# First chunk of a Mamba-2 scan with a maxout FFN: B by token turned on TensorE instead of loaded, x in two transfers, and every engine's order rewritten

## The chip, the cores and the metric

The kernel runs on one core of a Trainium2 chip. A core has TensorE (PE; its weight loads are a row of their own, PEld), VectorE (DVE), ScalarE (ACT), GpSimd (POOL), and SyncE (SP), which here issues nearly all DMAs. Every engine works through its own list of instructions in order, and waits at an instruction until the semaphores that it needs have come. The metric is device microseconds of one execution; the kernel before has a median of 245.2 us in 3 runs.

## The reference, cut to what matters

The first part is a scan over 768 tokens for 4 batches x 8 heads (head width 32, state width 16):

```python
for c in range(nc):                       # chunks of tokens
    cum = np.cumsum(log(a)[chunk])
    M = (C @ B.T) * exp(cum_i - cum_j) * causal
    y = M @ x + (C @ state) * exp(cum_i)
    state = exp(cum[-1]) * state + (B * exp(cum[-1] - cum_j)).T @ x
```

The second part takes the 3072 tokens with 256 channels (heads side by side) through a maxout layer: `h = max(y @ w1, y @ w2, y @ w3)` with 768 columns each, `out = h @ w_out`. The four weights come as 64-bit floats.

## The kernel before, in words

**Chunks.** The 768 tokens of each batch are six chunks of 128 tokens, each worked as two halves of 64 (`W`). A chunk of the scan gives y for 4 x 128 tokens; its FFN follows, mixed in with the scan of the next chunk. Chunk 0 is worked by code of its own (all names with `first_`), since nothing can run before it.

**The order is written out by hand.** `OPENING` is one list of words for chunk 0 and the preparation of the weights. `FIRST`, `SECOND`, `STEADY` and `LAST` are the lists for the chunks after it, 12 strings each, one for each unit of the up-projection (6 blocks of 128 columns x 2 products). Each word calls one function, which puts its instructions at the end of the engines' lists; a word with `+` continues a function that stopped at a `yield`. So the place of a word sets the order on each engine, and an engine whose next instruction waits lets everything behind it wait.

Words of `OPENING` that matter, with lines of the profile:

- `em` (L656, L662) decay from the middle of the chunk; `cm` (L666) C times that decay, "Cd0".
- `fj0`, `bt0` (L451, L458 to L466) the decay from each token to the end, turned to tokens on partitions; `R`, `S0`, `S1` (L385 to L405) the exponents of the decay between tokens, `x0` to `x3` (L418) their exp for each batch.
- `tC`, `tB` (L589) VectorE transposes C and B; `cp` (L676) copies C with every other head zeroed, in two halves, "CP"; `sc0` (L601) the scores; `p0` to `p3` (L607) scores times decay.
- `bT` (L617) turns the first 64 tokens of B back on TensorE; `bm` (L623) times the decay, "Bm"; `Am` (L637) the state in mid-chunk, `mid` (L645) its masked copy.
- `ya0` to `ya3` (L799, copy L814), `yc0` to `yc3` (L828, L799, copies L838 and L840): y of the first and of the second 64 tokens, put into `yT`. `yc` starts with Cd0 times mid (L828).
- `z` adds one filler product (L413) to the next bank of PSUM that is opened; fillers compute nothing that is used.
- `clip log run hl1 hl2` (L331, L336, L342, L482 to L489) make the running sums of log a for chunks 1 to 5, split in three bf16 parts. These go out to DRAM (`sums`, L492) and come back as `left` (L504, word `rows`) and `right` (L498), the operands of the exponents of chunk 1 (`X02`, `X24`, L522). `minus1` (L326) fills `right` with its constant rows on ScalarE. `fj`, `bt` (L352, L361) the decays to the end for chunks 1 to 5.
- `fetch` issues the next transfer of 512 KB of weights (L205); `decode` and `sign` turn its 64-bit words to fp32: two ScalarE operations (L224, L225), three on VectorE (L227, L230, L237), and one on POOL (L240).
- `bu0:1` and the like: next step of the difference of two weights ("d", L917) and of its splitting in parts ("wH", "wL", "wS", L865 to L905). `g` (L1067) turns a block of w2; with wo it makes "fold" (L1081).
- `m0` (L877) the first two up products with the first 64 tokens of each batch; `n0` and `n1` complete them; `n2` to `n11` (L1325) are the other up products of chunk 0, in plain fp32; `q` (L1108) its down products. From chunk 1 on the parts H, L and S are used (L981, L1022, L1140).
- `Bd0`, `A0` (L699, L714) the state at the end of chunk 0. It needs B by token for all 128 tokens, which `LB0` loads (L144, 256 KB in rows of 64 bytes).
- `y`, `v`, `Y` (L769, L790, L779): y of a later chunk; between its two parts ScalarE reads one column of the bank (`seen`), and the second part waits for that.

Before `OPENING`, the transfers of C and B of chunk 0 (L155, four each), one weight, x of chunk 0 in one piece, and two more weights (`NFETCH`) are issued in the text of the kernel:

```python
    load_first("C")
    load_first("B")
    fetch()
    load(0, "x")
    for _ in range(NFETCH):
        fetch()
```

In the plans, `Z` is one unit of the up-projection: it opens one of the two `up` banks of PSUM, finishes the unit before (`late`, L1022) and, for every second unit, VectorE takes the maximum (`h`, L1031) that frees the bank. `hS`, `wS` (L865), `hL` (L1044) are parts of h and of weights. `d` is a down product, `t`, `c`, `e`, `s`, `A` steps of the next chunk's scan, `X` and `W` its exponents, `E` their exp with the mask on POOL (L531, L536).

Of the kernel before, what the change touches and what calls it, by code (L numbers as in the profile page):

```python
# [20 lines left out]
def kernel(  # L21
# [20 lines left out]
    nc = tc.nc  # L42
# [25 lines left out]
    NFETCH = 2  # L68
# [79 lines left out]


# [544 lines left out]

    def scan_bd(c):
# [7 lines left out]
    def scan_state(c):  # L703
# [5 lines left out]
        for b in range(NB):  # L709
            for r in range(NP):  # L710
                h = b * NH + 2 * r
                for u in us:
# [3 lines left out]
                        lhsT=st["Bd"][rows, h:h + 2].rearrange("j h n -> j (h n)"),  # L716
# [498 lines left out]
    def first_word(w):  # L1215
# [21 lines left out]
        elif w == "bT":  # L1237
            first_turned_b()
# [73 lines left out]
    def first_group(n):  # L1312
# [36 lines left out]
    )  # L1349
    FIRST = [  # L1350
        "Z e 1 bu1:1 load bu1:1 1 bu1:1 bu0:1 bu1:1",
        "Z q X04 E E E bu0:1",
        "Z E q q t c 1",
        "Z q bo:1 bo:1",
        "Z bu1:1 s 1 1 1",
        "Z bu2:1 bu2:1 1 g",
        "Z bu2:1 bu2:1 G6 G6",
        "Z A 1",
        "Z r r r bu2:1 r W04 E E 1 bo:1 bo:1 bo:1 bo:1",
        "Z y d d",  # L1360
        "Z d d d E E d v Y 1",
        "Z 1 1 1 d d",
    ]
    SECOND = [
        "Z e d d t c bo:1 bo:1 d load d",
        "Z s",
        "Z 1 1 1 1 1 d d",
        "Z d d",
        "Z A 1",
        "Z d d",  # L1370
        "Z d 1 d",
        "Z W04 d E E",
        "Z d d d y v",
        "Z d d E E",
        "Z d d Y 1",
        "Z 1 1 d d 1",
    ]
    STEADY = [
        "Z 1 t d d d",
        "Z c E load d",  # L1380
        "Z d 1 d s 1",
        "Z 1 d 1 1 d A E",
        "Z d d",
        "Z d e d 1",
        "Z d d W04 E 1 1 E",
        "Z d y d d E",
        "Z E d v 1",
        "Z Y 1 1 d",
        "Z d 9 d d E E",
        "Z d 1 1 d",  # L1390
    ]
    LAST = [
        "Z d d",
        "Z d d d d d d",
        "Z d d",
        "Z d d",
        "Z d d",
        "Z d d d d",
        "Z l l",
        "Z l",  # L1400
        "Z l l l l",
        "Z l l l",
        "Z l l",
        "Z l l l",
# [33 lines left out]
    def act(c, word):  # L1438
# [77 lines left out]
        "R S0 S1 x0 x1 x2 x3 tC tB cp minus1 fj0 bt0 sc0 p0 p1 p2 p3 bT bm Am mid em cm ya0 ya1 ya2 ya3 yc0 yc1 yc2 yc3 m0 clip "  # L1516
        "log run hl1 hl2".split())
    for word in OPENING.split():
# [20 lines left out]
        elif word == "Bd0":  # L1539
            scan_bd(0)  # L1540
# [64 lines left out]
```

## Time and profile before

| | us |
|---|---|
| median of 3 runs (244.84 to 245.66) | 245.2 |
| the profiled execution | 246.31 |
| its span, first to last instruction | 244.6 |
| PE busy | 235.1 |
| DVE busy | 145.5 |
| ACT busy | 134.2 |
| POOL busy | 115.4 |

The profile is one execution. Rows give a start in us from the span's start, a length, the engine, the line of the kernel, the operation, what it writes and reads and the number of instructions merged in the row; in brackets the idle time of the engine ahead of it and what ended it. Rows of waits give total, times, longest. SPq is the issue of DMAs by SyncE. The profiled execution lies 1.1 us above the median; 1.7 us of it lie outside the span. DMA moved 17.88 MB in 70987 packets, of which 64460 were under 512 bytes.

### The profile page before, as it was taken

How to read it: one execution, taken by the hardware profiler on the slowest of the kernel's cores; microseconds unless marked ns; L12 is line 12 of the kernel's file. 1: busy time of each engine (PE TensorE's matmuls, PEld its weight loads, DVE VectorE, ACT ScalarE, POOL GpSimd, SP SyncE). 2: the span in 40 equal slices, each digit the busy share in tenths (PEclk: the TensorE clock that was granted, in tenths of full speed). 3: DMA queues.
4: the chain of work that ended last, by engine and by line, in shares of the span. 5: the costliest groups of instructions: out<-in, count | busy, mean ns of one | idle time of the engine just before them, and what ended most of it. 6: DMA issues, size and time to landing. Idle time of an engine off the chain costs nothing.

```text
span 244.6 us, 7115 instructions
## 1 busy us (share of the span) xinstructions
PE 235.1 (96%) x3024; PEld 186.6 (76%) x3024; DVE 145.5 (59%) x231; ACT 134.2 (55%) x254; POOL 115.4 (47%) x111
## 2 busy tenths in 40 slices
PE   8798999999989999999999999999999999999994
PEld 3456475566768878888878888888888888998993
DVE  5988998946698254787533963456764362333232
ACT  4788684903845474555547545663726364344352
POOL 5024566686696759374765323863315123122231
PEclk9889999999999999999999999999999999999999
DMA  3999996023939121290021450020000020002002
GB/s 84 206 352 381 150 184 138 3 46 62 126 68 136 12 87 36 62 128 4 0 91 40 93 69 3 3 82 6 0 3 3 3 88 0 0 0 88 1 1 86
DMA packets 70987, 17.88 MB, mean 73 GB/s; under 512 B 64460, under 2 KB 67884, under 8 KB 70956
## 3 DMA queue, kind: packets, MB, share of 16 engines
q1 hardware_dynamic: 70556, 17.19, 32.4%
q8 instruction: 23, 0.38, 0.6%
q10 hardware_dynamic: 400, 0.25, 0.3%
q14 instruction: 8, 0.07, 0.1%
HBM read 14.14 MB, written 3.29 MB: 71 GB/s over the span
## 4 chain that ended last, share of the span: by engine, by line
PE 90%; DVE 4%; issue 2%; DMA 1%; ACT 1%; SPq 1%; DVEq 0%; POOL 0%; POOLq 0%
PE up L981 22%; PE o L1140 19%; PE up L1022 11%; PE up L1325 7%; PE y L790 3%; PE o L1108 3%; PE near L1193 3%; PE y L769 3%; PE fold L1081 2%; PE s L748 2%; PE A L714 2%; PE up L877 2%; PE o L1121 1%; PE cross L1193 1%; PE up L966 1%
## 5 line engine op out<-in xcount | busy, mean ns | idle before, releaser
L1044 POOL TENSOR_TENSOR hL<-h,hH 128x512 fp32r<-128x512 f32 (+1 forms) x31 | 39.4, 1272 | 80.9 <-ACT hH L1043 79.7
L988 ACT ACTIVATE up<-up 128x512 f32<-128x512 f32 x60 | 35.3, 588 | 49.7 <-PE up L981 47.1
L865 DVE SCALAR_TENSOR_TENSOR hS<-hL,hH 128x512 fp32r<-128x512 f32 (+1 forms) x31 | 28.6, 921 | 31.1 <-POOL hL L1044 31.1
L981 PE MATMUL up<-yH,wH 128*128 128x512 f32 x116 | 39.5, 422 | 1.1 <-DVE h L1031 1.1
L1031 DVE SCALAR_TENSOR_TENSOR h<-up,m 128x512 f32<-128x512 f32 x29 | 20.0, 689 | 30.2 <-PE up L1022 28.1
L1022 PE MATMUL up<-yS,wS 128*128 128x512 f32 x116 | 36.6, 396 | 0.0
L981 PE MATMUL up<-yL,wL 128*128 128x512 f32 x116 | 36.0, 391 | 0.0
L240 POOL TENSOR_TENSOR w<-w_u,w_r 128x512 uint32<-128x512 uint32 x12 | 16.4, 1366 | 27.4 <-DVE w_r L237 27.4
L1027 ACT COPY m<-up 128x512 f32<-128x512 f32 x29 | 17.0, 586 | 18.9 <-PE up L1022 17.1
L1022 PEld LDWEIGHTS up<-yS,wS 128*128 128x128 f32 x116 | 21.4, 188 | 6.0 <-ACT up L988 1.1
L981 PEld LDWEIGHTS up<-yL,wL 128*128 128x128 f32 x116 | 21.8, 188 | 5.0
L536 POOL TENSOR_SCALAR_AFFINE_SELECT L<-L 64x1024 f32<-64x1024 f32 x16 | 19.8, 1235 | 6.7 <-ACT L L531 6.1
L1043 ACT ACTIVATE hH<-h 128x512 fp32r<-128x512 f32 (+1 forms) x31 | 19.0, 611 | 6.4 <-DVE h L1031 4.6
L981 PEld LDWEIGHTS up<-yH,wH 128*128 128x128 f32 x116 | 18.0, 190 | 4.0 <-issue 1.4
L1325 PE MATMUL up<-yT,d 128*128 128x512 f32 x40 | 18.6, 600 | 0.0
L1140 PE MATMUL o<-wH,hH 128*128 128x256 f32 x96 | 15.9, 287 | 0.3 <-issue 0.3
L1140 PEld LDWEIGHTS o<-wH,hH 128*128 128x128 f32 x96 | 14.2, 189 | 2.2 <-issue 0.7
L1140 PE MATMUL o<-wL,hL 128*128 128x256 f32 x96 | 15.4, 283 | 0.0
L756 DVE TENSOR_TENSOR L<-s,L 128x512 f32<-128x512 f32 x20 | 12.7, 682 | 3.5 <-PE s L748 3.5
L1140 PE MATMUL o<-wS,hS 128*128 128x256 f32 x96 | 14.2, 284 | 0.0
L1140 PEld LDWEIGHTS o<-wS,hS 128*128 128x128 f32 x96 | 13.2, 190 | 0.8
L1140 PEld LDWEIGHTS o<-wL,hL 128*128 128x128 f32 x96 | 13.3, 191 | 0.2
(189 smaller groups left out, 417.0 us busy)
## 6 DMA issues: line engine op xcount, KB each, us to landing
raw_x<-in_x_dram SPq DMA_DIRECT2D x6, 512.0 KB
out_dram<-ob SPq DMA_DIRECT2D x11, 256.0 KB
rb<-in_moe_w_dram SPq DMA_DIRECT2D x5, 512.0 KB
early<-in_moe_w_dram SPq DMA_DIRECT2D x4, 512.0 KB
rb<-in_moe_w_out_dram SPq DMA_DIRECT2D x3, 512.0 KB
raw_B<-in_B_dram SPq DMA_DIRECT2D x5, 256.0 KB
runs_C<-in_C_dram SPq DMA_DIRECT2D x32, 32.0 KB
runs_B<-in_B_dram SPq DMA_DIRECT2D x32, 32.0 KB
```

The costliest lines, as they stand in the source:

```text
L240: nc.gpsimd.tensor_tensor(out=t.rearrange("p k f -> p (k f)").bitcast(U32), in0=u, in1=r, op=ALU.add)
L536: nc.gpsimd.affine_select(out=part, in_=part, pattern=[[0, 2], [0, NH], [1, W]], compare_op=ALU.is_ge, fill=0.0, base=0, channel_multiplie ...
L865: nc.vector.scalar_tensor_tensor(out=out, in0=L, scalar=-RAISE, in1=H, op0=ALU.mult, op1=ALU.add)
L981: nc.tensor.matmul(out=bank, lhsT=up_parts[q, i][z][:, k, g * P:(g + 1) * P], rhs=y_parts[c][z][:, k], start=(z == 0 and k == 0), stop=(z ...
L988: nc.scalar.mul(bank, bank, RAISE + 1.0)
L1022: nc.tensor.matmul(out=up, lhsT=up_parts[q, i][2][:, k, g * P:(g + 1) * P], rhs=y_parts[c][2][:, k], start=False, stop=(k == KD - 1), skip ...
L1027: nc.scalar.copy(out=m, in_=up)
L1031: nc.vector.scalar_tensor_tensor(out=h, in0=up, scalar=0.0, in1=held["m"], op0=ALU.max, op1=ALU.max)
L1043: nc.scalar.mul(H, h, NEAR)
L1044: nc.gpsimd.tensor_tensor(out=L, in0=h, in1=plain(H), op=ALU.subtract)
L1140: nc.tensor.matmul(out=o[b // 2][:, b % 2], lhsT=left[:, b * P:(b + 1) * P], rhs=right, start=(first and b % 2 == 0), stop=True, skip_grou ...
L1325: nc.tensor.matmul(out=p, lhsT=of(k), rhs=yT[0][:, k], start=(k == 0), stop=(k == KD - 1))
```

## The change

1. B of chunk 0 by token is no longer loaded (`LB0` is gone). `bT` now turns all 128 tokens on TensorE, and ScalarE copies the result to SBUF; `whole_bd` multiplies it on POOL with the decay, whose layout is changed to fit, and `A0` reads it in that layout.
2. x of chunk 0 comes as two transfers of 64 tokens.
3. The transfers are words of `OPENING` now: C, B, two weights, both halves of x, two weights, and so on.
4. `OPENING` and the plans are rewritten; `STEADY` is replaced by `THIRD` and `FOURTH`, so each chunk has its own. There are 16 fillers `z` where there were 24.

```diff
+    def first_rows_of_x(u):
+
+        src, w = sources["x"]
+        if u == 0:
+            blocks[0]["x"] = whole([P, BH, w], "raw_x")
+        rows = slice(u * W, (u + 1) * W)
+        nc.sync.dma_start(
+            out=blocks[0]["x"][rows], in_=src[:, :, rows, :].rearrange("b h s n -> s (b h) n"))
...
-    load_first("C")
-    load_first("B")
-    fetch()
-    load(0, "x")
-    for _ in range(NFETCH):
-        fetch()
...
-        from_j[0] = const.tile([P, BH], FP32, name="from_j0")
+        from_j[0] = const.tile([P, NP, NB, 2], FP32, name="from_j0")
         nc.vector.tensor_copy(
-            out=from_j[0].rearrange("p (b h) -> p b h", h=NH), in_=rows[:, 1])
+            out=from_j[0], in_=rows[:, 1].rearrange("p b (r g) -> p r b g", g=2))
...
-        tp = bank_[0:W]
         for r in range(NP):
-            nc.tensor.transpose(
-                out=tp[:, r], in_=blocks[0]["BT"][:, r, 0:W], identity=ident)
-        held["B_tp"] = tp
+            nc.tensor.transpose(out=bank_[:, r], in_=blocks[0]["BT"][:, r], identity=ident)
+        held["B_tp"] = bank_[0:W]
+        yield
+        blocks[0]["B"] = t = half([P, NP, HN], "raw_B")
+        nc.scalar.copy(out=t, in_=bank_)
...
+    def whole_bd():
+
+        st = blocks[0]
+        st["Bd"] = Bd = half([P, NP, HN], "Bd")
+        nc.gpsimd.tensor_tensor(
+            out=Bd.rearrange("p r (c n) -> p (r c) n", n=N),
+            in0=st["B"].rearrange("p r (c n) -> p (r c) n", n=N),
+            in1=from_j[0].rearrange("p r b g -> p (r b g)").unsqueeze(2)
+            .to_broadcast([P, BH, N]), op=ALU.mult)
...
     OPENING = (
-        "fetch z z z z z em fj0 fj0+ z z z z z bt0 R R+ cols clip tC em+ cm log run tB cp hl1 cp+ hl1+ S1 bt0+ S0 decode decode+ sign x3 sc0 x0 p3 z z bT x1 fetch p0 z z z z ya0 p1 bm x2 ya1 hl2 p2 hl2+ hl2+ z Am mid z yc0 yc2 yc1 minus1 decode decode decode+ sign yc0+ yc1+ yc2+ fetch fetch fetch yc3 yc3+ ya3 ya2 ya3+ sign+ fetch sign+ z z z z z g decode decode decode bu0:1 decode z m0 "
...
+        "fC minus1 z z z z z em cols em+ R R+ S1 fj0 fj0+ fB fetch clip log tC cm cp S0 x0 tB cp+ bt0 decode bt0+ z bT bT+ Bd0 run hl1 x1 decode+ x2 sign fetch decode x3 bm sc0 p0 fj p2 fx0 z z Am mid decode+ fx1 z z z z z yc0 yc2 z z z ya0 yc0+ ya2 sign hl1+ p3 ya3 p1 hl2 sign+ sign+ yc3 hl2+ fetch fetch fetch fetch ya1 yc1 g bu0:1 decode decode+ sign sign+ bt bt+ yc1+ yc2+ ya3+ yc3+ m0 decode bu0:1 decode+ hl2+ decode "
+        "n0 "
+        "n1 "
+        "n2 g+ decode+ "
+        "n3 sign sign+ sign A0 LB1 bu0:1 t fetch n0+ n1+ rows X02 decode sign+ g t+ 1 decode+ sign E bu1:1 n2+ E fetch fetch X24 LC1 sign+ e decode decode n3+ E decode+ sign fetch "
+        "n4 q q Lx1 sign+ decode+ bu1:1 "
...
-        "Z e 1 bu1:1 load bu1:1 1 bu1:1 bu0:1 bu1:1",
+        "Z X04 E bu1:1 bu0:1 bu0:1 bu1:1",
...
-        plan = FIRST if c == 1 else SECOND if c == 2 else STEADY if c < NC - 1 else LAST
+        plan = (None, FIRST, SECOND, THIRD, FOURTH, LAST)[c]
```

More of the change, by code (lines that the diff above doesn't have):

```diff
@@ L67 @@
     RAISE = 2.0 ** 12
-    NFETCH = 2
     MASKED = -32768.0
@@ L715, in scan_state @@
                         out=As[u][r * PN:(r + 1) * PN, b].rearrange("p g d -> p (g d)"),
-                        lhsT=st["Bd"][rows, h:h + 2].rearrange("j h n -> j (h n)"),
+                        lhsT=(st["Bd"][rows, r, b * PN:(b + 1) * PN] if c == 0 else
+                              st["Bd"][rows, h:h + 2].rearrange("j h n -> j (h n)")),
                         rhs=st["x"][rows, h:h + 2].rearrange("j h d -> j (h d)"),
@@ L1237, in first_word @@
         elif w == "bT":
-            first_turned_b()
+            run(0, w, first_turned_b())
+        elif w in ("fC", "fB"):
+            load_first(w[1])
+        elif w in ("fx0", "fx1"):
+            first_rows_of_x(int(w[2]))
         elif w == "bm":
@@ L1335 @@
     OPENING = (
[13 rows of a table removed]
[13 rows of a table added]
     )
     FIRST = [
-        "Z e 1 bu1:1 load bu1:1 1 bu1:1 bu0:1 bu1:1",
[L1352 to L1362, printed above, removed]
+        "Z X04 E bu1:1 bu0:1 bu0:1 bu1:1",
+        "Z g E E",
+        "Z E t q",
+        "Z e 1 c",
+        "Z q s 1 1 1 1",
+        "Z bo:1 bo:1 bo:1 A bu2:1 load",
+        "Z bu2:1 bu2:1 G6 1 1 G6",
+        "Z r bu2:1 bu2:1 W04 E E",
+        "Z y v E bo:1 bo:1 bo:1 r r r",
+        "Z E Y d",
+        "Z 1 1 1 d 1 d d d",
+        "Z d",
     ]
     SECOND = [
-        "Z e d d t c bo:1 bo:1 d load d",
-        "Z s",
-        "Z 1 1 1 1 1 d d",
-        "Z d d",
-        "Z A 1",
-        "Z d d",
[L1371 to L1376, printed above, removed]
-    ]
[L1378 to L1382, printed above, removed]
-        "Z d d",
[L1384 to L1390, printed above, removed]
+        "Z t c e 1 d",
+        "Z d d d d d",
+        "Z d bo:1 bo:1 s 1 d 1 load d",
+        "Z 1 d",
+        "Z d d d",
+        "Z A 1 1 1",
+        "Z W04 E E d d E E",
+        "Z y v d",
+        "Z d d",
+        "Z Y 1",
+        "Z 1 1 1 d d",
+        "Z d d d",
+    ]
+    THIRD = [
+        "Z t load d d c d",
+        "Z d s 1 1",
+        "Z 1 A",
+        "Z d d d 1",
+        "Z d e 1 1 1",
+        "Z d",
+        "Z d d",
+        "Z d W04 E E",
+        "Z y v",
+        "Z d d d d d d d",
+        "Z Y 1 1 1 1 d d d",
+        "Z d d",
+    ]
+    FOURTH = [
+        "Z E E t d d",
+        "Z c d d d",
+        "Z d d",
+        "Z d d",
+        "Z d d s",
+        "Z 1 1 d d d d 1",
+        "Z A d e 1 1 1 d",
+        "Z d d",
+        "Z y v",
+        "Z d d",
+        "Z Y 1 1 1 1",
+        "Z d d",
     ]
     LAST = [
-        "Z d d",
         "Z d d d d d d",
+        "Z d",
+        "Z d d d",
         "Z d d",
@@ L1397 @@
         "Z d d",
-        "Z d d d d",
+        "Z d d",
+        "Z d d",
+        "Z l l l l l l",
         "Z l l",
-        "Z l",
-        "Z l l l l",
-        "Z l l l",
+        "Z l l l l l",
         "Z l l",
-        "Z l l l",
     ]
@@ L1515 @@
     firsts_of = frozenset(
-        "R S0 S1 x0 x1 x2 x3 tC tB cp minus1 fj0 bt0 sc0 p0 p1 p2 p3 bT bm Am mid em cm ya0 ya1 ya2 ya3 yc0 yc1 yc2 yc3 m0 clip "
+        "R S0 S1 x0 x1 x2 x3 tC tB cp minus1 fj0 bt0 sc0 p0 p1 p2 p3 bT fC fB fx0 fx1 bm Am mid em cm ya0 ya1 ya2 ya3 yc0 yc1 yc2 yc3 m0 clip "
         "log run hl1 hl2".split())
@@ L1539 @@
         elif word == "Bd0":
-            scan_bd(0)
+            whole_bd()
         elif word == "A0":
```

19 rows, old and new, of the table OPENING are left out of this document.

## The prediction

> **What bounds the kernel now.** I read the page's engine line first, then busy time by stretches, then TensorE's waits.
>
> ```profile
> PE 235.1 (96%) x3024; PEld 186.6 (76%) x3024; DVE 145.5 (59%) x231; ACT 134.2 (55%) x254; POOL 115.4 (47%) x111
> ```
> ```profile
> 7.20:10.60 3.40, 1.62 (x20) 0.42 (x18) 3.20 (x10) 2.25 (x5) 0.00 (x0) 1.00 1.00 230
> 10.60:14.00 3.40, 3.36 (x68) 2.45 (x68) 2.64 (x5) 3.40 (x8) 1.27 (x1) 0.50 1.13 248
> 28.80:43.50 14.70, 14.63 (x95) 8.58 (x94) 13.29 (x21) 10.05 (x19) 8.49 (x7) 1.00 0.85 145
> 54.00:73.00 19.00, 17.63 (x320) 12.78 (x319) 14.83 (x19) 10.01 (x20) 14.05 (x11) 1.00 0.52 85
> 90.00:240.00 150.00, 149.41 (x1939) 130.06 (x1938) 75.86 (x108) 78.57 (x148) 64.35 (x56) 1.00 0.16 35
> 240.00:244.60 4.60, 1.07 (x9) 0.86 (x8) 1.27 (x3) 0.66 (x2) 0.00 (x0) 1.00 0.34 114
> ```
> ```profile
> PE up L981 <- DVE h L1031: 1.1, 1, 1.1
> ```
> ```profile
> PE up L877 <- issue: 0.7, 1, 0.7
> PE y L769 <- ACT seen L779: 0.5, 2, 0.2
> ```
>
> The columns of a stretch are its length, busy time of PE, PEld, DVE, ACT and POOL, granted TensorE clock, DMA share, GB/s. TensorE is the bound: from 90 to 240 us it lacks 0.6 us, from 28.8 to 43.5 us 0.07. The last stretch is the tail after its last matmul, which the change leaves alone. No reordering can win inside a full TensorE. Two things can move: **when TensorE starts the dense up-projection products of chunk 0**, and its single waits afterwards (1.1 us for an up bank, 0.5 us in two waits for `seen`). Ahead of the dense part there is a chain over all engines, and between 10.6 and 14.0 us the clock is granted at 0.50, after a stretch in which TensorE was busy 1.62 of 3.40 us.
>
> The reference point is the dense part's start and the end of its first four groups:
>
> ```profile
> 20.77 0.67 PE L877 MATMUL up<-yT,d 128*128 128x256 f32 x2
> 22.16 3.18 PE L877 MATMUL up<-yT,d 128*128 128x256 f32 x14 [0.73 <-issue]
> 25.18 3.60 PE L1325 MATMUL up<-yT,d 128*128 128x512 f32 x8
> 28.62 0.59 PE L514 MATMUL e<-mask,ident 128*128 128x512 bf16 x2
> 29.14 0.41 PE L522 MATMUL e<-right,left 32*64 32x512 bf16 x4
> ```
>
> Products start at 20.77, stall 0.73 us, and n0 to n3 end at 28.78 (25.18 + 3.60). I work out both points for the changed order.
>
> **The change, part by part: the opening.** Engines work in order, so I walk their lists with these rows.
>
> ```profile
> 8.24 0.82 DVE L342 TENSOR_TENSOR_SCAN opening<-opening,lg 96x64 f32<-96x64 f32 x4
> 8.99 1.07 DVE L589 STREAM_TRANSPOSE BT<-first_B 128x512 f32<-128x512 f32 x1
> ```
> ```profile
> 9.10 0.41 ACT L482 CAST hl<-opening 96x256 bf16<-96x256 f32 x1 [0.55 <-DVE opening L342]
> 9.41 0.72 ACT L676 ACTIVATE CP<-CT,parity 128x512 f32<-128x512 f32 x1
> 10.04 0.66 ACT L224 ACTIVATE w_u<-early 128x512 f32<-128x512 f32 x1
> 10.61 0.66 ACT L225 ACTIVATE w_r<-early 128x512 f32<-128x512 uint32 x1
> 11.18 0.57 ACT L418 ACTIVATE L<-spread 128x512 f32<-128x512 f32 x1
> ```
> ```profile
> 11.54 0.69 DVE L237 SCALAR_TENSOR_TENSOR w_r<-early,w_r 128x512 uint32<-128x512 uint32 x1
> ```
> ```profile
> 18.63 1.26 POOL L240 TENSOR_TENSOR w<-w_u,w_r 128x512 uint32<-128x512 uint32 x1 [5.05 <-DVE w_r L237]
> ```
>
> Up to C's transpose and Cd0 nothing moves: VectorE does the same work in another order, and `minus1`, now on ScalarE at about 4.1 us, fits where ScalarE waits for E0. *B's transpose* moves ahead of the four scans: from 8.99 to 8.24, done 9.3. *ScalarE*: CP's first half, b0's exp (0.57), CP's second half, done 9.7 against 10.13; the cast no longer stands between. *TensorE*: B's four turns at 9.35, then the scores at 9.95 (before 10.2). Turning 128 instead of 64 columns of weights changes the weight load, not the moving columns; I cost it at nothing. *First decode*: ScalarE 9.7 to 10.9, VectorE 1.5 us behind (10.70, when `w_u` was there, to 12.23, by the rows): done 11.9. The copy of B by token (0.57 by ScalarE's spacing, 10.04 to 10.61) goes at 10.84, the cast at 11.4, two exps to 12.8, second decode to 13.9, the last exp to 14.4, and from there the four exps of `fj`. This copy is the one new wait on ScalarE (for B's turns, over at 10.0); were it late, cast, exps and decodes behind it would slip one for one. `Bd0` moves up on POOL to 11.45, as long as another POOL word by estimate (1.26), so the first weight is whole at 14.1 instead of 13.2 by this list; d asks for it at 18, which hides it.
>
> ```profile
> 14.62 0.67 DVE L623 TENSOR_TENSOR Bm<-B_tp,mid_j 64x512 f32<-64x512 f32 x1
> 15.22 0.67 DVE L607 TENSOR_TENSOR L<-s,L 128x512 f32<-128x512 f32 x1
> 15.81 0.41 DVE L489 TENSOR_TENSOR hl<-sums_rest,hl 96x256 bf16<-96x256 f32 x1
> 16.73 0.42 DVE L645 TENSOR_TENSOR mid<-A,parity 128x256 f32<-128x256 f32 x1 [0.51 <-PE A L637]
> ```
> ```profile
> 16.01 0.65 PE L637 MATMUL A<-raw_x,Bm 64*32 64x64 f32 x32
> 16.60 0.39 PE L413 MATMUL y<-mask,ident 128*128 128x512 bf16 x1
> 17.21 0.49 PE L828 MATMUL y<-Cd,mid 32*64 32x64 f32 x32 [0.23 <-DVE mid L645]
> 17.63 1.44 PE L799 MATMUL y<-L,raw_x 64*32 64x64 f32 x96
> ```
>
> *State path*: Bm 11.85 to 12.5 (before 14.62). A needs x's first half. Two fillers wait for the bank of b1's exp (12.3); at the same 0.50 clock A runs 13.15 to 14.25 (twice 0.65, partly at full clock), mid 14.3 to 14.7: 2.4 us earlier. *VectorE behind it*: second decode to 16.1, the sums' rest 0.41, then the two held-back weights p3 and p1 (spaced 0.6, as 14.62 to 15.22) to 17.7, `hl` 0.41, d 18.05 to 18.7; POOL's word for d is ready at 17.4 (16.1 + 1.26). *TensorE*: the last 32 products of x with p1's weights follow, a third of 1.44, to 18.2. The fillers are 16 now, 24 before; those left run while TensorE waits for p3 and cost nothing.
>
> ```profile
> 30.36 0.39 PE L361 MATMUL from_js_tp<-ident,fj 96*128 96x96 f32 x2
> 30.82 0.63 PE L1067 MATMUL w2T_tp<-ident,w 128*128 128x128 f32 x4
> ```
>
> Then `g` (0.63, the next instruction 0.46 after its start) and `bt` (0.39), which before came at 30.36: first up product at **19.1**, against 20.77. The copy of yT that it waits for stands on ScalarE behind the third decode and ends at about 18.8. Eight products of 0.227 (3.18/14) end at 20.9; yT's late columns are copied on VectorE by 20.95, behind the third decode (1.5 from d's end at 18.7) and three small copies, 0.7 in all by estimate from `hl`'s 0.41; eight more to 22.75, n2 and n3 3.60 to **26.35**, against 28.78: 2.43 us, of which 0.73 is a stall that I don't expect again (it waited for nothing shown; 0 to 0.73, and I take 0 as no engine is named). With `bt` done already: **2.8 us**.
>
> **DMA.**
>
> ```profile
> 3.52 2.13 DMA first_C<-in_C_dram
> ```
> ```profile
> L205 SPq DMA_DIRECT2D early<-in_moe_w_dram x4: 462/469/4047, 6.0 to 11.6; - x4
> ```
> ```profile
> L144 SPq DMA_DIRECT2D raw_B<-in_B_dram x6: 381/2564/2633, 25.7 to 138.6; - x6
> ```
> ```profile
> 15.38 0.68 ACT L224 ACTIVATE w_u<-early 128x512 f32<-128x512 f32 x1 [0.93 <-DMA early<-in_moe_w_dram]
> ```
> ```profile
> 19.83 2.56 SPq L504 DMA_DIRECT2D left<-sums  x3
> 22.49 2.35 SPq L498 DMA_DIRECT2D right<-sums  x3
> ```
>
> The issue behind x (many short rows) was held 4.05 us, one behind a raw B or C about 2.56. Before, the second weight stood behind x and was waited for until 15.38; now two weights go ahead of x, so it is there before 12.7. x in halves is next: the same bytes as before ahead of its end, needed at 13.1 and 14.9 instead of 15.1; I take it as in time (0 to 0.6 late). Dropping chunk 0's raw B takes away 256 KB that nothing near waited for: nothing gained by itself. What gets worse is **`right`**. SP now puts the sums' stores, raw B of chunk 1 and a weight ahead of `left` and `right`. `hl` is ready at 18.1; store 18.5, raw B 18.9, the weight held to 21.5, `left` to 24.0, `right` to 26.4, landed near 28.0 (last issue's start plus C's 2.13). Behind 26.35 stand A (0.65), four turns (0.5) and two mask products (0.5): TensorE asks at 27.9; before it came at 29.14 without a wait. Between 0 and 1.6 (if the weight is held 4.05), I take 0.3.
>
> **The later plans.** Products, downs and copies are the same in number. In the new order down products stand between chunk 1's y and the `seen` wait, and base products in the next: 0.5 gone. The up bank's wait, 1.1: between two `h` VectorE now has C's and B's transposes, `hS` and Cd, but no longer a `wL`; 0 to 1.1 may remain, I take half. Against that, four rewritten plans can open new waits; the nearest row, 0.6 over 150 us, gives the size of one: 0.55.
>
> Sum: -2.8 + 0.3 - 0.5 - 0.55 + 0.55 = **-3.0 us**. Against its own time the profiled execution of 246.3 us (span 244.6) becomes 243.3; that run lies 1.1 above the median of 245.2, so I forecast **242.2**. Best end: no clock dip (A 0.6 earlier), no wait for `right` (0.3), all the later ones gone without new ones (1.1): 240.2. Worst end: x 0.6 late, `right` 1.6, the up bank's wait kept (0.55): 244.6.
>
> **The clock.** The row says that a stretch with 1.62 of 3.40 us busy was followed by 3.4 us at 0.50. By my walk 7.2 to 10.6 now holds about 2.2 us busy, so the dip may vanish; I keep it. The Trainium skill ("TensorE: Matmul & The Clock Gate", "What's actually happening") says that a free-running window of 3413 ns decides the clock; the trace's stretch agrees with that length. Its Part 4 ("PE-mode transpose") says that a transpose does not count as TensorE being busy. That speaks against this change: by it B's and fj's turns drop out and the window counts 1.3 us, so the dip stays, as in my sum. No row before shows the rule apart.
>
> **Rivals.**
> *A, `right` late* (9%): the weight held 4.05 as behind x: 1.3 more than my sum, 243.5. For: SP's list; against: raw B held others 2.56.
> *B, a second slow stretch* (9%): with 8 fewer fillers 10.6 to 14.0 counts as sparse and 14.0 to 17.4 also runs at 0.50: remaining fillers and 0.49 of Cd products double, and the y products end behind p1: first up product 20.3, time 243.4. Against: the walk has TensorE busy some 2.7 of 3.4 us there.
> *C, new VectorE waits in the plans of chunks 1 to 4* (23%): every time an up bank's `h` stands behind a slow queue, TensorE loses 1.1, as in the row. The gain without later waits is 2.5 (2.8 - 0.3). Two or three extra waits end within the noise; from three up, 3.3 and more, it is slower: with four 4.4 - 2.5, 247.1. For: VectorE is busy 14.83 of 19.00 us in that stretch and one such wait exists; against: 0.6 us lost in 150.
> *D, it does nothing* (3%): the opening's gain is given back because VectorE's decodes, busy 13.29 of 14.70 us, feed n4 too late: 245.2. Against: d for n4 is ready at 29.5, asked for at 30.4.
>
> **How the numbers follow.** Forecast 56%. Noise is 0.3%, 0.74 us, about what a measurement can tell. Faster: 56 + 8 + 8 = 72; same: 7 of C, 3 of D, 1 each of A and B: 12; slower: 16 of C. The range leaves out C's slower part and a little at the low end: 240.5 to 245.4.
>
> **What would show it.** Right: first up product near 19, n3 done near 26.4, no up wait of 1 us near 70. Wrong: a wait of TensorE for `right` above 1 us, clock 0.50 beyond 14, DVE waits of `h` in chunks 2 to 4, or B's scores later than 10.2.

## The result, and the profile after

The changed kernel takes 244.21 us (median of 10 runs, 243.41 to 245.46); the kernel before, run beside it, 245.75 (10 runs). The ratio is 0.9934, 95% interval 0.9905 to 0.9964. It is faster, as forecast, by about half of what was forecast. The profiled execution took 244.52 us (span 242.8), against 246.31 (span 244.6).

The engine line and the same stretches as before, in the changed kernel (the columns are those of the prediction):

```profile
PE 232.0 (96%) x3016; PEld 183.7 (76%) x3016; DVE 149.6 (62%) x231; ACT 133.4 (55%) x255; POOL 115.7 (48%) x111
```
```profile
7.20:10.60 3.40, 2.33 (x47) 1.03 (x39) 2.96 (x9) 3.07 (x9) 0.00 (x0) 1.00 0.91 282
10.60:14.00 3.40, 1.75 (x82) 1.13 (x67) 2.94 (x6) 3.40 (x8) 1.88 (x2) 1.00 1.14 178
28.80:43.50 14.70, 13.72 (x62) 7.61 (x60) 14.42 (x20) 12.03 (x22) 8.58 (x7) 1.00 0.99 232
54.00:73.00 19.00, 18.12 (x328) 13.65 (x326) 11.18 (x15) 10.76 (x21) 13.04 (x12) 1.00 0.69 106
90.00:240.00 150.00, 149.22 (x1796) 129.76 (x1794) 81.21 (x112) 79.13 (x151) 61.54 (x53) 1.00 0.17 37
```

The clock is full from 10.6 to 14.0 us, where before it was half. From 28.8 to 43.5 TensorE is now idle for 0.98 us; before it lacked 0.07. TensorE's waits name the places:

```profile
PE up L995 <- DVE h L1045: 1.3, 1, 1.3
...
PE s L762 <- DVE Cd L696: 0.9, 1, 0.9
PE up L891 <- DVE d L931: 0.9, 1, 0.9
PE e L524 <- DMA right<-sums: 0.4, 1, 0.4
```

The timeline of TensorE around the start of the dense part:

```profile
19.42 1.99 PE L891 MATMUL up<-yT,d 128*128 128x256 f32 x8
22.28 1.89 PE L891 MATMUL up<-yT,d 128*128 128x256 f32 x8 [0.86 <-DVE d L931]
24.00 3.60 PE L1343 MATMUL up<-yT,d 128*128 128x512 f32 x8
27.53 0.65 PE L727 MATMUL A<-raw_x,Bd 128*32 128x64 f32 x32
...
29.58 0.41 PE L524 MATMUL e<-right,left 32*64 32x512 bf16 x4 [0.38 <-DMA right<-sums]
```

The first up product starts at 19.42 (before 20.77, forecast 19.1), and n3 ends at 27.60 (24.00 + 3.60; before 28.78, forecast 26.35). A stall is there again, 0.86 us in the middle of the sixteen first products. One gain nobody had forecast is in the groups of the y products, first of the kernel before, then of the changed one:

```profile
L790 PE MATMUL y<-L,raw_x 64*32 64x64 f32 x640 | 8.3, 224 | 0.0
L769 PE MATMUL y<-Cd,S 32*64 32x64 f32 x320 | 6.9, 223 | 0.5 <-ACT seen L779 0.5
```
```profile
L804 PE MATMUL y<-L,raw_x 64*32 64x64 f32 x640 | 7.4, 225 | 0.0
L783 PE MATMUL y<-Cd,S 32*64 32x64 f32 x320 | 6.9, 223 | 0.0
```

The same 640 products take 0.9 us less where `y` and `v` stand side by side, and the two waits for `seen` (0.5) are gone, as forecast.

### The profile page after: what moved, and what is told of

It reads as the page before. It is cut to its first block, busy times and chain, and to the rows that moved or that the text cites. A ratio compares the mean times of both kernels' runs of the same rounds, so it can differ in the third digit from the quotient of the medians.

```text
span 242.8 us, 7096 instructions
## 1 busy us (share of the span) xinstructions
PE 232.0 (96%) x3016; PEld 183.7 (76%) x3016; DVE 149.6 (62%) x231; ACT 133.4 (55%) x255; POOL 115.7 (48%) x111
## 4 chain that ended last, share of the span: by engine, by line
PE 78%; SPq 6%; DMA 5%; DVE 4%; issue 2%; ACT 2%; POOL 0%; DVEq 0%; ACTq 0%; POOLq 0%
PE up L995 23%; PE o L1154 19%; PE up L1036 11%; DMA rb<-in_moe_w_dram 3%; PE near L1207 3%; PE up L1343 3%; PE y L804 3%; PE o L1122 3%; PE y L783 3%; SPq L213 2%; PE fold L1095 2%; PE s L762 2%; DMA early<-in_moe_w_dram 2%; SPq L163 2%; PE cross L1207 2%
## 5 line engine op out<-in xcount | busy, mean ns | idle before, releaser
L1041 ACT COPY m<-up 128x512 f32<-128x512 f32 x29 | 17.0, 587 | 21.8 <-PE up L1036 20.5
L1154 PE MATMUL o<-wS,hS 128*128 128x256 f32 x96 | 13.3, 283 | 0.0
```

Source lines behind the costliest of these rows:

```text
L1041: nc.scalar.copy(out=m, in_=up)
L1154: nc.tensor.matmul(out=o[b // 2][:, b % 2], lhsT=left[:, b * P:(b + 1) * P], rhs=right, start=(first and b % 2 == 0), stop=True, skip_grou ...
```

## The experiments

All ratios are to the kernel before, run on the same chip beside each kernel. Theory: the opening starts the dense part earlier, and most of that is given back at once (a stall, the wait for `right`, the wait for Cd), so that the gain lies in the plans. Rival: the opening carries the gain, and the plans are about neutral.

### Each part alone: old_opening, old_plans

old_opening is the kernel before with the plans `FIRST` to `LAST` of the changed one (seven words added at the end of `OPENING`, which the new plans expect to be done: two y steps, two down products, three steps of weights); old_plans is the changed kernel with the plans of before (two y steps at the end of `OPENING` are left to the plans).

```diff
-        plan = FIRST if c == 1 else SECOND if c == 2 else STEADY if c < NC - 1 else LAST
+        plan = (None, FIRST, SECOND, THIRD, FOURTH, LAST)[c]
```

> The kernel before with its own opening, and the changed kernel's lists for chunks 1 to 5 (with two more down products, three more weight steps and two more y steps at the opening's end, which the new lists expect done). Theory P (the plans carry the gain, by fewer changes between kinds of product: y's products with x take 0.8 us less in the changed kernel, and the waits for the one-column read and a few small ones go): about 1.2 us under the kernel before, ratio 0.995. Theory O (the prediction's: the gain comes from the earlier dense start of chunk 0): within 0.3 us of the kernel before, ratio 0.999 to 1.001.

> The changed kernel's opening with the lists for chunks 1 to 5 of the kernel before (two y steps at the opening's end are left to the next list, as it was before). Theory P: the opening alone gives 1.6 us (first products 1.35 earlier, the 0.4 us turn of the decays already done), and gives back 0.4 at the wait for `right` and 0.9 at chunk 1's scores, so about 0.4 to 0.6 us under the kernel before, ratio 0.998. Theory O: 1.5 us or more under it, ratio 0.994 or lower.

old_opening: 244.37 us, 0.9939 [0.9908, 0.9971]. old_plans: 247.8 us, 1.0063 [1.0033, 1.0094]. In this set the new plans alone give all of the gain (a second set, opening_again below, gives a smaller ratio); the new opening with the old plans loses 1.6 us by the ratio. Old plans behind the new opening open two waits that neither kernel had, for `m` and for `yS`:

```profile
PE up L995 <- DVE h L1045: 1.3, 1, 1.3
PE up L995 <- ACT m L1041: 1.2, 1, 1.2
...
PE up L1036 <- DVE yS L874: 0.4, 1, 0.4
```

### The load of B that was dropped: b_loaded

The changed kernel, but chunk 0's B by token is loaded again, ahead of `LB1`, and ScalarE's copy is gone.

```diff
-        "n3 sign sign+ sign A0 LB1 bu0:1 t fetch
+        "n3 sign sign+ sign LB0 Bd0 A0 LB1 bu0:1 t fetch
```

> The changed kernel, but chunk 0's B by token is loaded as before (64 tokens turned on TensorE for mid-chunk, no copy on ScalarE; the load issued just ahead of chunk 1's raw B). The prediction said that dropping this load gains nothing by itself: then the time is that of the changed kernel, ratio 0.993 to 0.995, with TensorE's wait for `right` still 0.4 us. The rival says that the load's room in SyncE's list is the gain: each raw B holds the next issue 2.5 to 4.8 us, so `left` and `right` come 2.5 us later, and TensorE waits about 3 us there: 2.5 us over the changed kernel, ratio 1.003 to 1.006.

246.32 us, 0.9999 [0.9967, 1.0032]: the whole gain is gone. SP's timeline shows why, and TensorE's waits where it lands:

```profile
18.11 6.00 SPq L143 DMA_DIRECT2D raw_B<-in_B_dram  x2
...
28.32 1.79 SPq L500 DMA_DIRECT2D right<-sums  x3
```
```profile
PE e L524 <- DMA right<-sums: 2.9, 1, 2.9
```

Two raw B keep SP for 6.0 us, and `right`, issued behind them, makes TensorE wait 2.9 us instead of 0.4. The seven of its ten executions with a mean clock of 0.997 or more still have a median of 246.07, so the loss isn't one of the clock.

### SP's order: rows_early, rows_mid

In the changed kernel the weight behind raw B of chunk 1 is held for 4.84 us, and `left` and `right` stand behind it:

```profile
18.48 0.47 SPq L143 DMA_DIRECT2D raw_B<-in_B_dram  x1
19.00 4.84 SPq L213 DMA_DIRECT2D rb<-in_moe_w_dram  x1
23.95 2.36 SPq L506 DMA_DIRECT2D left<-sums  x3
26.36 1.79 SPq L500 DMA_DIRECT2D right<-sums  x3
```

rows_early puts `left` and `right` ahead of raw B and the weight; rows_mid ahead of the weight alone.

```diff
-        "n3 sign sign+ sign A0 LB1 bu0:1 t fetch n0+ n1+ rows X02
+        "n3 rows sign sign+ sign A0 LB1 bu0:1 t fetch n0+ n1+ X02      (rows_early)
+        "n3 sign sign+ sign A0 LB1 bu0:1 t n0+ n1+ rows fetch X02      (rows_mid)
```

> The changed kernel with `left` and `right` issued ahead of chunk 1's raw B and of a weight. Theory S (SyncE's list makes `right` late: the weight behind raw B is held 4.8 us): the wait of TensorE for `right`, 0.4 us in one profile and 1.1 in another, goes, 0.4 to 1.0 us under the changed kernel, ratio 0.989 to 0.992. Rival: raw B now comes late for its turns, which stand ahead of the same products, and TensorE waits as long there: ratio 0.993 to 0.996.

> The changed kernel with SP's issue of one weight moved from ahead of the sums' two loads (left, right) to behind them; raw B of chunk 1 stays ahead of both. Theory that right comes late because the weight issued between raw B and the loads is held for 4.8 us: without it the hold behind raw B falls on left, 4.8 us from 19.0, so left goes at 23.8, right at 26.2, and right lands near 27.9 to 28.2 instead of 29.6; TensorE's wait for right (0.4 to 1.1) goes; the weight that is put back goes at 28.6 instead of 23.8 and is asked for later than that. Time 0.4 to 1.0 below the changed kernel, ratio 0.990 to 0.992. Rival: the weight now comes late for its decode, VectorE's decodes slip, and TensorE waits for d or for Cd by 1 us or more: ratio 0.996 to 1.002.

rows_early: 247.52 us, 1.004 [1.0006, 1.0074]. The wait for `right` goes, and a larger one takes its place:

```profile
PE trB L559 <- DMA raw_B<-in_B_dram: 3.2, 1, 3.2
```

Part of this loss is one of the clock: the stretch of that wait (29.53 to 32.94, TensorE busy 1.71 of 3.41 us) is followed by 3.41 us at half clock, and 11 of the 12 executions have a mean clock of 0.993 or less.

rows_mid: 245.25 us, 0.9974 [0.9951, 0.9996]. The wait for `right` is gone too, but `left` starts no earlier: at 24.05, where it started at 23.95. By the profile SP waits here for something else, the stores of the sums, which must have landed before `left` can read them:

```profile
SPq L506 <- DMA sums<-hl: 4.8, 1, 4.8
```

In rows_early, with nothing between the stores and `left`, this wait is 4.24 us and `left` starts at 22.75. So the held weight isn't the only thing that makes `left` late; in the changed kernel the stores have landed when the weight's hold ends (SP then waits 0.03 us). Neither expectation names this. In the trace of rows_mid the stall in the first up products (1.5) and the wait for Cd (1.2) grew as well. In both runs the rival's wait came (raw B; Cd by 1 us or more), and rows_early lost more than its rival said.

### x in one transfer, and fewer fillers: x_whole, fillers_less

```diff
-        rows = slice(u * W, (u + 1) * W)
+        if u:
+            return
+        rows = slice(0, P)                                             (x_whole)
...
-        yc0 yc2 z z z ya0
+        yc0 yc2 ya0                                                    (fillers_less)
```

> The changed kernel with x of chunk 0 in one transfer. The state of mid-chunk starts at 13.7 us; x whole should land near 14.3. Theory N (halves are worth nothing: the y products wait for the last weights p3 and p1 until 17.8 anyway): within 0.3 us of the changed kernel, ratio 0.993 to 0.995, with a wait for x of 0.3 to 0.8 us. Rival (the delay passes on, one for one): 0.6 us more, ratio 0.996.

> The changed kernel without the three fillers ahead of `ya0`. In both kernels TensorE stalls for 0.7 to 0.9 us behind its 348th product, near 21.4 us. Theory I (TensorE's instructions themselves come late): the stall stays behind the 348th product, so three products later in the program, behind the third of the second eight, at about the same time of 22.2. Theory D (the profile's releaser: a wait for the second d): it stays between the first and the second eight products, and ends with d. Time: as the changed kernel by both, within 0.3 us; the clock stays at 1.00 if TensorE's busy share of the window 14 to 17.4 us suffices, else 0.5 to 1.2 us more.

x_whole: 243.81 us, 0.9929 [0.9899, 0.9959], so splitting x is worth nothing that can be measured, though in its trace, which has two stretches at half clock, A waits 1.7 us for x (expected 0.3 to 0.8). fillers_less: 244.18 us, 0.9914 [0.988, 0.9949], equal to the changed kernel as well. What it tells is the place of the stall:

```profile
19.18 2.64 PE L891 MATMUL up<-yT,d 128*128 128x256 f32 x11
22.28 1.24 PE L891 MATMUL up<-yT,d 128*128 128x256 f32 x5 [0.46 <-issue]
```

Three fillers less, and it stands behind eleven up products instead of eight: behind the 348th product of the program in both. It belongs to a place in the list of instructions, and neither `d` nor a bank is its cause.

### VectorE's order at 70 us: h_first

From 69.6 to 73.3 us VectorE works `hS` (1.60), Cd (1.62) and then the maximum `h`, for which TensorE waits 1.25 us. h_first asks for `h` ahead of Cd.

```diff
-        "Z e 1 c",
-        "Z q s 1 1 1 1",
+        "Z e c",
+        "Z 1 q s 1 1 1 1",
```

> The changed kernel; in chunk 1 the step that makes Cd is taken one unit later, so that on VectorE the maximum `h` of the second pair stands ahead of Cd. In the changed kernel TensorE waits 1.25 us there for the up bank, while Cd and `hS` before it take 1.6 us each beside POOL's masks. Theory Q (VectorE's order makes this wait): the wait falls below 0.3 us, about 1.0 to 1.2 us under the changed kernel, ratio 0.988 to 0.990. Rival (POOL sets it: `hS` waits for `hL` behind the masks, whatever follows): the wait stays at 0.8 us or more, ratio 0.992 to 0.994.

243.24 us, 0.9894 [0.9862, 0.9925], span 241.9. The wait for `h` is gone and no other took its place; the time is 1.0 us below the changed kernel's, as the theory said.

### Cd of chunk 1: cd_early, cd_sooner

Cd stands on VectorE behind a decode whose weight lands late (37.95) and whose three operations take 1.4 to 1.6 us each instead of 0.4 to 0.7 while GpSimd works; Cd then ends at 43.7 and the scores wait 0.88. cd_early asks for Cd one unit earlier, cd_sooner ahead of that decode.

```diff
-        "n6 t+ q e+ sign decode decode+ n4+ g+ sign decode q decode+ n5+ fetch "
-        "n7 sign+ sign+ bu2:1 c c+ sign E 1 bd n6+ s 1 n7+ "
+        "n7 sign+ 1 sign+ bu2:1 c c+ sign E bd n6+ s 1 n7+ "                              (cd_early)
+        "n6 t+ q e+ sign decode decode+ n4+ g+ sign 1 decode q decode+ n5+ fetch "        (cd_sooner)
+        "n7 sign+ sign+ bu2:1 c c+ sign E bd n6+ s 1 n7+ "                                (cd_sooner)
```

> The changed kernel; chunk 1's Cd is made ahead of the last step of a weight's decode on VectorE instead of behind it. The scores of chunk 1 wait 0.9 us for Cd, since it holds the bank that they write. Theory Q: the wait falls below 0.2 us and the time by 0.7 to 0.9 us, ratio 0.990 to 0.991. Rival (the decode is late instead, and the products of n10 wait for their weights' difference): ratio 0.993 to 0.996.

> The changed kernel with one unit of VectorE's queue asked for earlier in the opening's list, so that chunk 1's Cd product stands ahead of the decode that had stretched to 1.5 us beside GpSimd; by the same shift of one unit, h comes ahead of Cd later in chunk 1, as in h_first. Theory that TensorE's 0.9 us wait of chunk 1's scores for Cd comes from what is queued ahead of it on VectorE: Cd is done near 40 instead of 43.7, the wait is under 0.3, and with the up bank's wait gone too the time is 1.8 to 2.2 below the changed kernel, ratio to before 0.984 to 0.987. Rival (seen in the run that moved Cd by one decode operation): the wait moves to the next thing that hangs on the late weight, and the time stays at that of h_first, ratio 0.989 to 0.991.

cd_early: 244.18 us, 0.9948 [0.992, 0.9976]: Cd still stands behind two of the three operations, at 41.85, and the scores wait 1.4 us (the profile names CP). cd_sooner: 243.45 us, 0.9889 [0.9855, 0.9923], span 241.4. Cd now starts at 38.93 on VectorE, and the 0.9 us wait is gone:

```profile
38.93 0.69 DVE L696 TENSOR_TENSOR Cd<-trC,E 128x512 f32<-128x512 f32 x1 [0.64 <-PE trC L559]
39.53 0.42 DVE L235 TENSOR_SCALAR w_u<-w_u 128x512 f32<-128x512 f32 x1
```

`h` did not move there (its wait of 1.2 us stayed), so the side effect that the expectation names didn't come.

### The orders together: all3, two

all3 is cd_sooner, h_first and rows_mid in one; two leaves rows_mid out.

> The changed kernel with three orders mended together: Cd of chunk 1 ahead of the late decode, h ahead of Cd later in chunk 1, and the weight's issue behind left and right. If the three waits (0.4, 0.9 and 1.25 us) are separate and nothing takes their place, the time is 2.0 to 2.6 us below the changed kernel, ratio 0.982 to 0.986, and the chain's only wait left near 20 to 45 us is the stall of TensorE that waits for nothing shown. Rival: the weight that is put back comes later for the decodes that Cd and the later units hang on, and one of the waits comes back at 1 us or more: ratio 0.988 to 0.993.

> The changed kernel with two orders mended: Cd of chunk 1 ahead of the decode of the late weight (as in cd_sooner), and h ahead of Cd later in chunk 1 (as in h_first); SP's order is left alone. If TensorE's waits for Cd (0.9) and h (1.25) are separate terms, neither is left, the time is 1.8 to 2.3 us below the changed kernel, and the ratio to before 0.983 to 0.987. Rival: with both gone TensorE meets the next late item (the bank of an up product at 44 us, as with three mends, or the next h), and the ratio stays at 0.988 to 0.991, that of either alone.

all3: 243.19 us, 0.9892 [0.9857, 0.9927]. The three waits are gone, but the profiled execution opens with a stretch of half clock (first up product at 20.90), and a new wait of 0.5 for an up bank stands at 45 us. two: **242.5 us, 0.9884 [0.9853, 0.9915]**, span 240.5, the fastest of all. Neither wait is left in its trace (a wait of 0.31 us for an up bank stands at 43 us), and TensorE needs 213.48 us from its sixteenth up product to its last, against 215.06: 1.6 us less, where the two waits were 2.1. Whether the two terms add up in full is not settled, by this or by the ratio, whose interval takes in both expectations.

### Where y's two parts stand: y_split, y_joined

y_split puts `v` into the unit behind `y` again in chunks 1 to 4 of the changed kernel. y_joined does the opposite to the kernel before, in chunks 1, 3 and 4.

```diff
-        "Z y v d",
-        "Z d d",
+        "Z y d",
+        "Z v d d",                                                     (y_split, chunk 2)
...
-        "Z d y d d E",
-        "Z E d v 1",
+        "Z d d d E",
+        "Z y v E d 1",                                                 (y_joined, chunks 3 and 4)
```

> The changed kernel with the two parts of each chunk's y products (those by Cd and state, and those by L and x) put into neighbouring units again instead of one behind the other, in chunks 1 to 4. Theory that 0.8 us of the gain comes from these 1024 products taking 7.07 us together instead of 7.89 us: they take 7.7 to 7.9 again, and the time is 0.5 to 0.8 above the changed kernel, ratio 0.996 to 0.998. Rival: the 0.8 us is how the profile books the ends of pipelined products, and the time is that of the changed kernel, ratio 0.992 to 0.995.

> The kernel before with one edit: in chunks 1, 3 and 4 the two parts of the y products (those by Cd and state, those by L and x) stand in one unit, one right behind the other, as chunk 2 has them already. Theory that this order is itself a term of the gain: the L products take 7.4 us of busy time instead of 8.3, and two waits for seen of 0.25 go; time 0.8 to 1.4 below before, ratio 0.994 to 0.997. Rival: without the new distances between y, seen and the copies a wait for seen or for Y takes the place of the switches, ratio 0.998 to 1.002.

y_split: 246.26 us, 1.0017 [0.9984, 1.005], 2 us more than the changed kernel. The L products take 8.3 us again, and a wait for `seen` of 1.2 us comes with it. y_joined: 246.15 us, 1.002 [0.9991, 1.0049]. The products get shorter there too (7.6 us), but this comes up:

```profile
96.02 1.30 PE L790 MATMUL y<-L,raw_x 64*32 64x64 f32 x106
98.39 0.42 PE L790 MATMUL y<-L,raw_x 64*32 64x64 f32 x22 [1.07 <-issue]
```

So the order of y is needed for the gain and doesn't give it alone: what stands around it decides whether a wait takes its place.

### The same kernels once more: before_again, before_third, opening_again, after_again

No edit, further traces, because the trace of before had half clock near its start.

> The kernel before, unchanged, for a second trace. Theory that half of the opening's forecast gain was the half clock of that one execution: without it A runs at full speed, the first up product starts at 19.3 to 20.1 instead of 20.77, and n0 to n3 end at 27.3 to 28.2 instead of 28.78, so the new opening (27.53) gains 0 to 0.7 there. Rival: the old opening's chain is bound by ScalarE and VectorE, the clock of TensorE costs it little, and the first up product stays at 20.5 to 20.8. If the execution has the half clock again, it tells nothing of this.

> The old opening with the new plans, unchanged from old_opening, for a second trace. By the theory that the half clock made up the opening's gain: first up product 19.3 to 20.1 (20.83 in the execution with half clock), stall behind the 348th product 0.7 to 1.4, span 242.4 to 243.0, within 0.5 of the changed kernel. Rival: 20.5 or later, span 243.5 or more.

> The kernel before, unchanged, one more trace. Theory that the opening varies from one execution to the next (the trace with equal span was 0.9 under its kernel's median): n0 to n3 end at 28.0 or later with the clock at full speed, and from there to TensorE's end it takes 0.5 to 1 us longer than in the changed kernel. Rival: n0 to n3 end near 27.6 again and the part behind them varies instead.

> The changed kernel, unchanged, one more trace. By the theory that its first trace was a slow execution (244.52, median 244.2): n0 to n3 end at 27.0 to 27.5, span 241.8 to 242.6, with the waits for Cd (0.9) and h (1.25) at their places again. Rival: 27.5 and a span of 242.8 again.

before_again had the clock at full speed throughout the opening. Its timeline:

```profile
20.05 0.59 PE L877 MATMUL up<-yT,d 128*128 128x256 f32 x2
20.98 3.18 PE L877 MATMUL up<-yT,d 128*128 128x256 f32 x14 [0.34 <-issue]
24.00 3.60 PE L1325 MATMUL up<-yT,d 128*128 128x512 f32 x8
```

And before_third's, at full clock too:

```profile
19.86 0.67 PE L877 MATMUL up<-yT,d 128*128 128x256 f32 x2
21.75 3.18 PE L877 MATMUL up<-yT,d 128*128 128x256 f32 x14 [1.22 <-issue]
24.77 3.60 PE L1325 MATMUL up<-yT,d 128*128 128x512 f32 x8
```

At full clock the old opening ends n0 to n3 at 27.60, 28.37 and, in opening_again, 27.87 (28.78 in the first trace), the new one at 27.60 and 27.28. So the theory of before_again and opening_again holds, and the rival (20.5 or later at full clock) doesn't. All traces of these kernels side by side, in us; the last product's end is that of TensorE's timeline:

| execution | first up product | sixteenth ends | from there to the last product | span |
|---|---|---|---|---|
| before (half clock 10.6 to 14.0) | 20.77 | 25.35 | 215.72 | 244.6 |
| before_again | 20.05 | 24.16 | 215.13 | 242.8 |
| before_third | 19.86 | 24.93 | 215.67 | 245.7 |
| old_opening (half clock from 11.0) | 20.83 | 26.03 | 214.40 | 244.0 |
| opening_again | 19.66 | 24.43 | 214.43 | 242.4 |
| after | 19.42 | 24.17 | 215.06 | 242.8 |
| after_again | 19.43 | 23.84 | 215.20 | 242.6 |

before_again has 245.16 us (8 runs; ratio 0.999 [0.9951, 1.0028]), opening_again 244.33 (0.9969 [0.9938, 0.9999]); the profiled executions took 247.43 (before_third) and 244.33 (after_again). 5.1 us of before_third's span lie behind its last product, 3.5 in the others. Of 100 executions of the kernel before, run beside the first fourteen experiments, 79 have a mean clock of 0.997 or more and a median of 245.5, and 21 one of 0.993 or less and 247.0. Nine of the changed kernel's ten runs have 0.998 or more and a median of 244.16, 1.3 us under those 79.

## Why the prediction was right in direction and wrong in size

**The opening, -2.8: this is the step that failed.** It was a difference of two ends of n3, 28.78 and 26.35, and both were off. The first comes from an execution that ran 3.4 us at half clock, and I took it as the kernel's own; the three traces of the old opening at full clock end n3 at 27.95 on average. That is 0.8 of the forecast 2.4. The second came later than the walk has it, at 27.44 on average of two traces: 0.3 by the first up product (19.42 and 19.43 for 19.1), and 0.7 by the stall. What is left is 0.5 us, and `bt`'s 0.39 has been done: 0.9 instead of 2.8. (Five more traces at full clock, of kernels with the same opening, end n3 between 26.86 and 27.42.) Taking the run's 1.1 us above the median off the forecast as well kept the half clock's share as gain.

**The stall, taken as 0: failed.** It is part of the step above: I let 0.73 us go because no engine was named. It came again with 0.86 and 0.53 us, behind the same instruction. The cause is argued from the times in the last section; that it is a place in TensorE's list is shown by fillers_less.

**`right`, +0.3: about right in size, by luck.** 0.38 and 0.50 measured, 0.66 to 0.86 in h_first, old_plans and y_split, which have the same opening. The weight was held 4.84 us, not 2.56, and `right` landed at 29.58 instead of 28.0, but TensorE came for it at 29.20 instead of 27.9, so both errors cancel. The walk also gave the sums' stores no time to land, for which SP waits 4.8 us in rows_mid. That dropping raw B is "nothing gained by itself" was wrong: b_loaded costs 2.1 us. The prediction counted who waits for those bytes and not who stands behind them on SP, which it did do for rival A.

**The waits for `seen`, -0.5: right. The up bank, -0.55: wrong**, 1.25 us are left; I said that Cd stands between the two `h` now, and h_first shows that this is the wait. **New waits, +0.55: about right in size** (Cd, 0.88), found in chunk 1 and not in the later plans, where none came. **Missing altogether:** y's two parts side by side, 0.9 us.

Put together: -0.9 (opening) +0.4 (`right`) -0.5 (`seen`) +0.1 (up bank) +0.9 (Cd) -0.9 (y) gives -0.9, the medians' difference is -1.54. The 0.6 between them lies within what single traces of one kernel differ by (before's spans: 242.8 to 245.7), and is not assigned.

**The parts.** By the medians old_opening and its second run give the new plans 1.3 to 1.5 us, by the ratios 0.8 to 1.5; the changed kernel against old_opening (244.21 against 244.37 and 244.33) gives the new opening about nothing, by the ratios at most 0.9. Its earlier start is paid back by the waits for `right` and Cd, which stand in the 0.7 us that TensorE needs more behind the sixteenth product (215.06 and 215.20 against 214.40 and 214.43). Of rival A the condition came (the weight held over 4.05 us), its price did not. B did not come in the changed kernel's traces, but it can: in y_split, with the same opening, 14.58 to 17.99 ran at half clock and the first up product came at 20.42 (B said 20.3). D did not come as told, though the wait for Cd does come from VectorE's decodes. C, new waits in later plans, is what old_plans shows for the mixed kernel, not for the changed one.

**The clock.** The dip is gone from this trace, where I kept it. It can come again: two stretches of TensorE's window length, in all3 and in x_whole, show what it hangs on.

```profile
10.97:14.38 3.41, 1.31 (x52) 0.70 (x34) 3.21 (x6) 3.41 (x8) 2.16 (x2) 1.00 1.12 144
14.39:17.80 3.41, 3.41 (x64) 1.51 (x57) 3.16 (x8) 1.60 (x6) 1.67 (x2) 0.50 0.85 237
```
```profile
10.63:14.04 3.41, 1.18 (x42) 0.54 (x31) 2.58 (x6) 3.31 (x7) 1.53 (x2) 1.00 1.17 209
14.04:17.45 3.41, 1.83 (x34) 1.15 (x35) 1.36 (x4) 2.22 (x7) 1.02 (x1) 0.50 0.88 305
17.45:20.86 3.41, 3.41 (x69) 1.82 (x68) 2.62 (x7) 0.61 (x3) 1.39 (x1) 0.50 0.89 323
```

A stretch of 3.41 us with 1.31, 1.18 or (itself at half clock) 1.83 us of busy TensorE is followed by one at half clock. The Trainium skill ("TensorE: Matmul & The Clock Gate", "What's actually happening") says that the window is free-running, so that the place of the change varies from run to run; the traces agree, the stretches begin at another time in each execution. Busy time alone gives no sharp boundary: a stretch of y_split with 1.94 us (11.16 to 14.58) was followed by half clock, one near the changed kernel's end with 1.70 us (237.52 to 240.93) was not. The Trainium skill ("TensorE: Matmul & The Clock Gate", Part 4, "PE-mode transpose") says that a transpose "doesn't count as PE-busy the same way". The changed kernel's own window speaks against that, and the second row holds the four turns of B alone:

```profile
8.83:12.24 3.41, 2.05 (x69) 1.48 (x69) 2.77 (x10) 3.08 (x7) 0.12 (x1) 1.00 1.20 316
```
```profile
8.83:12.24 3.41, 0.66 (x4) 0.42 (x4) 1.00 1.20 316
```

Without the turns 1.39 us would be left, less than the 1.62 in the prediction's row that was followed by half clock; here full clock followed. Whether these turns run in the mode that the page means, no run here shows.

## What to carry to other kernels

Before a gain is sized as a difference of two times in one trace, see whether the reference execution is an ordinary one: look at the granted clock by stretches and at a second trace. A transfer that nobody waits for still has a price if it is issued ahead of one that somebody waits for. And an opening that starts earlier is worth only what the next late items (here `right`, Cd and a stall at a fixed instruction) let through: list them in the order of time before counting the gain.

## What the hardware showed that was not expected

**A stall at a fixed instruction.** Ahead of the 349th product TensorE stands still in 16 of the 20 traces, for 0.31 to 1.48 us; the profile names no engine for it, or one that fillers_less rules out. The DMA view shows a transfer of 0.02 MB on the queue of kind `instruction` there (window 19.9 to 21.0 of the changed kernel):

```profile
q8 instruction: 1, 0.02, 5.5%
```

In the records of that queue the transfer (16,384 bytes) starts at these times, and the stall ends so much later:

| | before | before_again | before_third | after | h_first | all3 | rows_mid | y_joined at 97 us |
|---|---|---|---|---|---|---|---|---|
| transfer starts | 19.77 | 18.68 | 19.31 | 19.98 | 19.24 | 21.06 | 20.82 | 96.12 |
| stall ends | 22.16 | 20.98 | 21.75 | 22.28 | 21.68 | 23.51 | 23.05 | 98.39 |
| difference | 2.4 | 2.3 | 2.4 | 2.3 | 2.4 | 2.5 | 2.2 | 2.3 |

Over the 16 traces it is 2.2 to 2.5 us. In the four without the stall TensorE came to the 348th product at least 1.9 us after the transfer's start. That it waits for its next instructions fits all of this, but no run changed that transfer, so it is argued and not shown. It would also say why the earliest start (two, 18.64) still has 0.9 us of it.

**A hold on SP.** The issue behind raw B, a transfer in short rows, was held 4.84 us in the changed kernel, 2.28 in rows_early and 2.60 in the kernel before (raw C, at 28.48). What makes it long or short was not tried.

**VectorE beside GpSimd.** Operations of 0.4 to 0.7 us took 1.4 to 1.6 (in the changed kernel the decode at 38.7 to 43.0 us, `hS` and Cd at 70 us):

```profile
71.10 1.62 DVE L696 TENSOR_TENSOR Cd<-CT,E 128x512 f32<-128x512 f32 x1
72.64 0.68 DVE L1045 SCALAR_TENSOR_TENSOR h<-up,m 128x512 f32<-128x512 f32 x1
```

That GpSimd causes it is read from the overlap alone, and was not tried.
